# Running the experts on half of the tokens at a time, the first half under the attention of the second

## The chip, the cores and the metric

The kernel runs on one core of a Trainium2 chip. The metric is the device time of the core in microseconds; the time before is 399.92 us, the median of three runs (399.46 to 400.68). A run of one core is called slow when it is more than 1.5% above the fastest run of the same kernel; ratios use the other runs alone.

In the profile, PE is TensorE (PEld its weight loads), DVE is VectorE, ACT is ScalarE, POOL is GpSimd and SP is SyncE, which here only issues DMAs. An engine's name with a q is its sequencer, which issues DMAs in program order. L405 is line 405 of the kernel in question.

## The reference

A block-sparse attention with 8 x 8 sorted blocks feeds a mixture of experts with one expert per token.

```python
# q, k, v: (4, 8, 768, 64) fp32;  sort_net: (4, 8, 8, 8);  8 blocks of 96 rows
P = sort_net
for _ in range(5):                      # alternating row and column normalisation
    P = P - P.max(-1); P = exp(P); P = P / P.sum(-1); P = P / P.sum(-2)
k_sorted = einsum('bhij,bhjcd->bhicd', P, k_blocks)     # v_sorted the same way
attn = softmax(q_blocks @ k_sorted^T / 8)               # each block against its own sorted block
x = (attn @ v_sorted) as (3072 tokens, 512)
for e in range(8):                      # domain_id: (3072,), about 384 tokens an expert
    out[domain_id == e] = relu(x[domain_id == e] @ w1[e]) @ w2[e]   # 512 -> 1024 -> 512
```

q, k and v are 18.9 MB of fp32, the weights 33.6 MB of fp32, the output 6.3 MB. The kernel computes in fp16.

## The kernel before

The attention works on 16 "pairs" (one batch, two heads). q, k and v are loaded by DMAs of GpSimd that cast to fp16 on the way. The result x stays in SBUF, transposed, four values of a token side by side. Only when all of it is there do the experts begin. For each expert, GpSimd gathers up to 448 columns of x with its own instruction, in two halves:

```python
def x_tr(p):                                   # attention, per pair
    ...                                        # 8 transposes on TensorE
    nc.scalar.copy(xT[:, b * 768:(b + 1) * 768, hp], o.rearrange("p i c -> p (i c)"))
# [cut: loads, tables of slots, scores, softmax]

def gather(e):
    xg = moe.tile([128, CAP, 4], FP16, tag="xg", name="xg")          # CAP = 448
    for s in range(2):
        nc.gpsimd.indirect_copy(xg[:, s * 224:(s + 1) * 224, :], xT, gidx[:, e, s * 14:(s + 1) * 14],
                                i_know_this_is_slow=True)
    return xg

def up(e, xg):
    for fc in range(8):
        ...
        for dc in range(4):
            nc.tensor.matmul(h_ps, w1e[:, dc, fc * 128:(fc + 1) * 128], xg[:, :, dc],   # stride of 4 elements
                             start=(dc == 0), stop=(dc == 3))
        nc.scalar.activation(hT[:, fc], h_ps, func=AF.Relu)

def put(o_ps, col):
    o_sb = ob.tile([128, 512], FP32, tag="osb", name="o_sb")
    nc.vector.tensor_copy(o_sb, o_ps)
    nc.gpsimd.indirect_dma_start(out, ..., o_sb, None, ...)          # scatter of 128 rows
# [cut: down, and a loop of further rounds for experts with more tokens than CAP; it runs zero times here]
```

The softmax here doesn't subtract the row's maximum and nothing guards it: scores larger than these inputs give would overflow.

Of the kernel before, what the change touches and what calls it, by code (L numbers as in the profile page):

```python
# [11 lines left out]
U16 = mybir.dt.uint16  # L12
# [6 lines left out]
NE, CAP, NC16 = 8, 448, 28  # L19
NTOK = 3072  # L20
OOB = 4096


@with_exitstack
def kernel(
# [12 lines left out]
    ORDERED = {ENG.PE, ENG.Activation, ENG.DVE, ENG.Pool}  # L38

    sm = ctx.enter_context(tc.tile_pool(name="sm", bufs=1))  # L40
    wpool = ctx.enter_context(tc.tile_pool(name="wp", bufs=5))
    keep = ctx.enter_context(tc.tile_pool(name="keep", bufs=1))

    gtab = nc.dram_tensor("gtab", (128, NC16), U16, kind="Internal")
    stab = nc.dram_tensor("stab", (128, NC16), I32, kind="Internal")


    xT = keep.tile([128, NTOK, 4], FP16, tag="xT")

    attn = ExitStack()  # L50
    stg = attn.enter_context(tc.tile_pool(name="stg", bufs=2))
# [3 lines left out]
    def loads(b, h0, h1, tiles):  # L55
        for src, t in zip((k, v, q), tiles):
            nc.gpsimd.dma_start(
                t[:, h0:h1, :],
                src[b, h0:h1].rearrange("h (p t) d -> p h (t d)", t=6),
            )  # L60

    def stage_tiles():
        return tuple(stg.tile([128, NH, 384], FP16, tag=t, name=t) for t in ("kst", "vst", "qst"))

    stage = {}


    sn = sm.tile([32, 64], FP32, tag="sn")
    nc.sync.dma_start(sn, sort_net.rearrange("b h i j -> (b h) (i j)"))
    d_raw = sm.tile([128, 48], I32, tag="draw")  # L70
    nc.sync.dma_start(d_raw, moe_domain_id.bitcast(I32).rearrange("(p x) -> p x", p=128))


    with tc.manual_schedule(engines={ENG.Pool}):
        stage[0] = stage_tiles()
        loads(0, 0, 2, stage[0])
        idf16 = sm.tile([128, 128], FP16, tag="idf16")
        make_identity(nc, idf16)
        loads(0, 2, 4, stage[0])
        iota_m = sm.tile([128, 128], I32, tag="iotam")  # L80
        nc.gpsimd.iota(iota_m, pattern=[[1, 128]], base=0, channel_multiplier=0)
        tri128 = sm.tile([128, 128], FP32, tag="tri128")
        make_upper_triangular(nc, tri128, 1.0, False)
        p_i = sm.tile([128, 1], I32, tag="pi")
        nc.gpsimd.iota(p_i, pattern=[[1, 1]], base=0, channel_multiplier=1)
        tok_i = sm.tile([128, 24], I32, tag="toki")
        nc.gpsimd.iota(tok_i, pattern=[[1, 24]], base=-1536, channel_multiplier=24)
        pos_i = sm.tile([128, 4, 6], I32, tag="posi")
        nc.gpsimd.iota(pos_i, pattern=[[1, 4], [16, 6]], base=-1536, channel_multiplier=4)
        loads(0, 4, 8, stage[0])  # L90
        stage[1] = stage_tiles()
        loads(1, 0, 8, stage[1])


    rs = sm.tile([32, 8], FP32, tag="rs")
    cs = sm.tile([32, 8], FP32, tag="cs")
    sn_ij = sn.rearrange("p (i j) -> p i j", j=8)
    sn_ji = sn.rearrange("p (i j) -> p j i", j=8)
    with tc.high_priority():
        for _ in range(5):  # L100
            nc.scalar.activation(sn, sn, func=AF.Exp)
            nc.vector.tensor_reduce(rs, sn_ij, axis=AX.X, op=ALU.add)
            nc.vector.reciprocal(rs, rs)
            nc.vector.tensor_tensor(sn_ij, sn_ij, rs.unsqueeze(2).to_broadcast([32, 8, 8]), op=ALU.mult)
            nc.vector.tensor_reduce(cs, sn_ji, axis=AX.X, op=ALU.add)
            nc.vector.reciprocal(cs, cs)
            nc.vector.tensor_tensor(sn_ji, sn_ji, cs.unsqueeze(2).to_broadcast([32, 8, 8]), op=ALU.mult)

        p_rep = sm.tile([32, 8, 8, 16], FP16, tag="prep")
        nc.vector.tensor_copy(p_rep, sn_ij.unsqueeze(3).to_broadcast([32, 8, 8, 16]))  # L110

        dmask = sm.tile([128, 16], FP16, tag="dmask")
        with nc.allow_low_precision("sums of one 1"):
            nc.vector.tensor_reduce(dmask, idf16.rearrange("p (j c) -> p c j", c=16), axis=AX.X, op=ALU.add)
        pt_ps = ps.tile([128, 8, 32], FP32, tag="av", bufs=2, name="pt_ps")
# [8 lines left out]
        def build_m(eng, a, b):  # L124
# [6 lines left out]
        build_m(nc.vector, 2, 8)  # L131
    build_m(nc.vector, 8, 16)
    build_m(nc.vector, 16, 32)


    iota_f = sm.tile([128, 128], FP32, tag="iotaf")
    nc.vector.tensor_copy(iota_f, iota_m)
    iota_h = sm.tile([128, 128], FP16, tag="iotah")
    nc.vector.tensor_copy(iota_h, iota_m)
    p4 = sm.tile([128, 1], I32, tag="p4")  # L140
    nc.vector.tensor_scalar(p4, p_i, 2, None, op0=ALU.arith_shift_right)
    p4f = sm.tile([128, 1], FP32, tag="p4f")
    nc.vector.tensor_scalar(p4f, p4, 80.0, None, op0=ALU.mult)

    pos_h = sm.tile([128, 24], FP16, tag="posh")
    nc.vector.tensor_scalar(pos_h, pos_i.rearrange("p a t -> p (a t)"), p4f, None, op0=ALU.add)
    tok_h = sm.tile([128, 24], FP16, tag="tokh")
    nc.vector.tensor_copy(tok_h, tok_i)
    dom_f = sm.tile([128, 24], FP32, tag="domf")
    nc.vector.tensor_copy(dom_f, d_raw.rearrange("p (j t) -> p j t", t=2)[:, :, 0])  # L150
    oh = sm.tile([128, NE, 24], FP32, tag="oh")
    nc.vector.tensor_tensor(oh, dom_f.unsqueeze(1).to_broadcast([128, NE, 24]),
                            iota_f[:, 0:NE].unsqueeze(2).to_broadcast([128, NE, 24]), op=ALU.is_equal)
    seg = sm.tile([128, NE, 24], FP32, tag="seg")
    nc.vector.memset(seg, 1.0)
    nc.vector.memset(seg[:, :, 0:1], 0.0)
    incl = sm.tile([128, NE, 24], FP32, tag="incl")
    nc.vector.tensor_tensor_scan(incl.rearrange("p e j -> p (e j)"), seg.rearrange("p e j -> p (e j)"),
                                 oh.rearrange("p e j -> p (e j)"), 0.0, op0=ALU.mult, op1=ALU.add)
    cnt = sm.tile([128, NE], FP32, tag="cnt")  # L160
    nc.vector.tensor_copy(cnt, incl[:, :, 23])
    ones_f = sm.tile([128, 1], FP32, tag="onesf")
    nc.vector.memset(ones_f, 1.0)
    rt_ps = ps.tile([128, 64], FP32, tag="av", bufs=2, name="rt_ps")
    nc.tensor.matmul(rt_ps[:, 0:NE], tri128, cnt, start=True, stop=True)
    nc.tensor.matmul(rt_ps[0:1, 32:32 + NE], ones_f, cnt, start=True, stop=True)
    base = sm.tile([128, NE], FP32, tag="base")
    nc.vector.tensor_copy(base, rt_ps[:, 0:NE])

    mx = sm.tile([1, 1], FP32, tag="mx")  # L170
    nc.vector.tensor_reduce(mx, rt_ps[0:1, 32:32 + NE], axis=AX.X, op=ALU.max)
    caps = sm.tile([1, 8], FP32, tag="caps")
    nc.vector.tensor_scalar(caps, iota_f[0:1, 0:8], float(CAP), float(CAP), op0=ALU.mult, op1=ALU.add)
    nc.vector.tensor_scalar(caps, caps, mx, None, op0=ALU.is_lt)
    extra_f = sm.tile([1, 1], FP32, tag="extraf")
# [324 lines left out]
```

## Time and profile before

| | before |
|---|---|
| median of the runs | 399.92 us |
| span of the profile | 398.7 us |
| first score matmul | 37.8 us |
| last x copy of the attention | about 136 us |
| experts | 138 to 391 us |
| PE busy | 236.3 us, 59% |

The page of the kernel before, part 1 (busy time and share of the span of each engine) and four rows of part 2. A row cuts the span into 40 equal slices of 10 us; each digit is the busy share in tenths, for PEclk the TensorE clock that was granted, and for DMA the mean of the 16 DMA engines.

```profile
PE 236.3 (59%) x1732; PEld 126.1 (32%) x1732; DVE 121.9 (31%) x324; ACT 106.9 (27%) x182; POOL 115.8 (29%) x138
...
PE   0034878887898305999209808910980994944950
...
POOL 8932456535700011140023214102311312212120
PEclk9999875557555556999757966985895797995995
DMA  8999619999997000017601661760100100100110
```

Read the rows together: from slice 14 on PE alternates between full and empty, and the DMA engines are mostly idle. The experts have neither TensorE nor the DMA engines as their limit.

Three groups of part 5 of that page. The columns are line, engine and operation, output and input with their shape and number, then busy us and mean ns of one, then the idle time of the engine just before them and what ended most of it.

```profile
L415 PE MATMUL h_ps<-xg,w1e 128*128 128x448 f16 x256 | 102.6, 574 | 98.7 <-POOL xg L405 98.7
...
L405 POOL INDIRECT_COPY xg<-xT,gidx 128x896 f16 x16 | 19.2, 1203 | 143.7 <-issue 143.7
L423 POOL DMA_INDIRECT out_dram<-o_sb,sidx x28 | 28.1, 1005 | 62.5 <-DMA out_dram<-o_sb,sidx 28.8
```

TensorE waits 98.7 us for gathered tokens. The gathers look cheap, 1.2 us each, but 143.7 us of GpSimd lie idle just before them, put down to "issue" (33.5 us before the first, 7.3 to 7.4 before each of the other fifteen). The timeline of GpSimd (start, duration, instruction, and in brackets the idle time before it) shows how that time lies:

```profile
152.44 1.19 POOL L405 INDIRECT_COPY xg<-xT,gidx 128x896 f16 x1 [7.34 <-issue]
160.96 1.19 POOL L405 INDIRECT_COPY xg<-xT,gidx 128x896 f16 x1 [7.32 <-issue]
169.47 1.19 POOL L405 INDIRECT_COPY xg<-xT,gidx 128x896 f16 x1 [7.32 <-issue]
170.85 1.12 POOL L423 DMA_INDIRECT out_dram<-o_sb,sidx  x1 [0.19 <-DVE o_sb L422]
174.51 1.02 POOL L423 DMA_INDIRECT out_dram<-o_sb,sidx  x1 [2.54 <-issue]
```

A gather costs 8.5 us of GpSimd, a scatter comes about 3.5 us after the one before. Two gathers and three and a half scatters per expert make 29.3 us, and eight experts 235 us. GpSimd is the limit of this stage, though its row shows it a fifth busy.

### The profile page before, as it was taken

What the parts mean: (1) busy time and instruction counts of PE and PEld (TensorE: products, weight loads), DVE (VectorE), ACT (ScalarE), POOL (GpSimd) and SP (SyncE); (2) the same over time, 40 slices, a digit from 0 to 9 for tenths busy, and PEclk for the clock granted to TensorE, in tenths of its full rate; (3) what the DMA queues carried; (4) which work ended last, traced back from release to release, by engine and by line L of the source; (5) the groups of instructions that cost most, each with busy time, mean ns of one, the idle gap of its engine ahead of it and who ended that gap; (6) DMA issues with size and microseconds to landing.
All of it is one profiled execution on the core that took longest, in us unless ns stands there. A gap on an engine that the chain in (4) does not pass through costs nothing. (4 is left out here: it accounts for less than half of the span.)

```text
span 398.7 us, 4513 instructions
## 1 busy us (share of the span) xinstructions
PE 236.3 (59%) x1732; PEld 126.1 (32%) x1732; DVE 121.9 (31%) x324; ACT 106.9 (27%) x182; POOL 115.8 (29%) x138
## 2 busy tenths in 40 slices
PE   0034878887898305999209808910980994944950
PEld 0023667676777201333002302300230231311320
DVE  6998877677766200011100200110020020020020
ACT  2001676677666501222002102200210210301300
POOL 8932456535700011140023214102311312212120
PEclk9999875557555556999757966985895797995995
DMA  8999619999997000017601661760100100100110
GB/s 112 187 179 161 87 3 178 209 210 194 190 198 124 0 0 2 0 53 132 96 9 59 121 114 53 125 101 5 54 28 0 69 9 28 60 0 26 51 55 28
DMA packets 30810, 32.98 MB, mean 83 GB/s; under 512 B 4671, under 2 KB 25151, under 8 KB 30784
## 3 DMA queue, kind: packets, MB, share of 16 engines
q0 software_dynamic: 27360, 32.51, 45.6%
q1 hardware_dynamic: 3424, 0.13, 0.6%
q8 instruction: 15, 0.25, 0.2%
q14 instruction: 11, 0.09, 0.1%
HBM read 52.53 MB, written 7.36 MB: 150 GB/s over the span
## 5 line engine op out<-in xcount | busy, mean ns | idle before, releaser
L415 PE MATMUL h_ps<-xg,w1e 128*128 128x448 f16 x256 | 102.6, 574 | 98.7 <-POOL xg L405 98.7
L417 ACT ACTIVATE hT<-h_ps 128x448 f16<-128x448 f32 x64 | 34.8, 544 | 206.9 <-PE h_ps L415 206.9
L422 DVE COPY o_sb<-o_ps 128x512 f32<-128x512 f32 x28 | 19.4, 692 | 232.0 <-PE o_ps L431 227.3
L415 PEld LDWEIGHTS <-w1e 128*128 128x128 f16 x256 | 30.0, 117 | 168.1 <-issue 167.5
L405 POOL INDIRECT_COPY xg<-xT,gidx 128x896 f16 x16 | 19.2, 1203 | 143.7 <-issue 143.7
L423 POOL DMA_INDIRECT out_dram<-o_sb,sidx x28 | 28.1, 1005 | 62.5 <-DMA out_dram<-o_sb,sidx 28.8
L431 PE MATMUL o_ps<-w2e,hT 128*128 128x512 f16 x192 | 42.9, 380 | 0.0
L348 ACT COPY xT<-x_ps 128x768 f16<-128x768 f16 x16 | 29.9, 1867 | 10.5 <-PE x_ps L347 10.3
L340 DVE TENSOR_TENSOR xr<-av_ps,rc 96x256 f16<-96x256 f32 x64 | 26.9, 421 | 2.2
L277 PE MATMUL kv_ps<-M,kvx 128*128 128x128 f16 x192 | 24.2, 291 | 4.9 <-DVE M L125 4.9
L263 POOL COPY kvx<-kst 128x768 f16<-128x768 f16 x16 | 13.7, 854 | 46.2 <-PE kv_ps L277 42.0
L431 PEld LDWEIGHTS <-hT 128*128 128x128 f16 x192 | 19.0, 99 | 25.3 <-issue 4.5
L277 PEld LDWEIGHTS <-kvx 128*128 128x128 f16 x192 | 17.3, 132 | 6.8 <-issue 4.9
L265 POOL COPY qx<-qst 128x768 f16<-128x768 f16 x16 | 14.2, 888 | 0.0
L356 POOL DMA_DIRECT2D w2e<-in_moe_w_dram x8 | 7.3, 908 | 22.8 <-PE o_ps L438 22.8
L264 POOL COPY kvx<-vst 128x768 f16<-128x768 f16 x16 | 13.3, 834 | 0.0
L347 PE MATMUL x_ps<-idf_86,xr 96*128 96x96 f16 x128 | 12.7, 267 | 0.6 <-DVE xr L340 0.6
L313 PE MATMUL v_ps<-idf_86,kvT_301 64*128 64x64 f16 x128 | 8.5, 221 | 7.4 <-ACT xT L348 7.4
L313 PE MATMUL v_ps<-idf_86,kvT_302 64*128 64x64 f16 x128 | 8.1, 219 | 7.6 <-ACT xT L348 7.6
L300 PE MATMUL q_ps<-idf_86,qx 128*128 128x128 f16 x96 | 12.5, 295 | 0.0
L339 DVE RECIPROCAL rc<-av_ps 96x4 f32<-96x4 f32 x64 | 11.0, 171 | 3.2 <-PE av_ps L336 2.8
L347 PEld LDWEIGHTS <-xr 96*128 96x128 f16 x128 | 10.6, 136 | 0.8 <-DVE xr L340 0.8
(129 smaller groups left out, 257.1 us busy)
## 6 DMA issues: line engine op xcount, KB each, us to landing
w1e<-in_moe_w_dram POOLq DMA_DIRECT2D x8, 1024.0 KB, 9.4
w2e<-in_moe_w_dram POOLq DMA_DIRECT2D x8, 1024.0 KB, 14.4
kst<-in_k_dram POOLq DMA_DIRECT2D x3, 768.0 KB, 7.2
vst<-in_v_dram POOLq DMA_DIRECT2D x3, 768.0 KB, 10.2
qst<-in_q_dram POOLq DMA_DIRECT2D x3, 768.0 KB, 14.0
out_dram<-o_sb,sidx POOLq DMA_INDIRECT x28, 2.7
kst<-in_k_dram POOLq DMA_DIRECT2D x2, 192.0 KB, 4.6
vst<-in_v_dram POOLq DMA_DIRECT2D x2, 192.0 KB, 5.8
```

What stands on the lines that cost most here:

```text
L265: nc.gpsimd.tensor_copy(qq, qs[:, h].rearrange("p h (t d) -> p t h d", d=D))
L277: nc.tensor.matmul(o[:, s].rearrange("p i c -> p (i c)"), kv[:, t, h], M[:, bh].rearrange("p i c -> p (i c)"), start=True, stop=True)
L313: nc.tensor.transpose(o[:, i], kt[r, c0:c0 + 128], idf16[r, r])
L340: nc.vector.tensor_tensor(xr[p][:, 4 * ih:4 * ih + 4, h * D:(h + 1) * D], o[0:BLK, :, 0:D], rc.unsqueeze(2).to_broadcast([BLK, 4, D]), op= ...
L347: nc.tensor.transpose(o[:, i], xr[p][:, i], idf16[0:BLK, 0:BLK])
L348: nc.scalar.copy(xT[:, b * 768:(b + 1) * 768, hp], o.rearrange("p i c -> p (i c)"))
L405: nc.gpsimd.indirect_copy(xg[:, s * 224:(s + 1) * 224, :], xT, gidx[:, e, s * 14:(s + 1) * 14], i_know_this_is_slow=True)
L415: nc.tensor.matmul(h_ps, w1e[:, dc, fc * 128:(fc + 1) * 128], xg[:, :, dc], start=(dc == 0), stop=(dc == 3))
L417: nc.scalar.activation(hT[:, fc], h_ps, func=AF.Relu)
L422: nc.vector.tensor_copy(o_sb, o_ps)
L423: nc.gpsimd.indirect_dma_start(out, bass.IndirectOffsetOnAxis(ap=sidx[:, col:col + 1], axis=0), o_sb, None, bounds_check=NTOK - 1, oob_is_ ...
L431: nc.tensor.matmul(o_ps, hT[:, fc, m * 128:(m + 1) * 128], w2e[:, fc], start=(fc == 0), stop=(fc == 7))
```

## The change

The intent is to take the gather off GpSimd and to use the DMA engines and TensorE, which idle in turns. x is now written to DRAM as rows, in two halves of 1536 tokens (batches 0 and 1, and batches 2 and 3). An expert's tokens of one half (at most 224 in a round) are fetched as rows by two DMA gathers and transposed on TensorE. Such a "unit" of half and expert needs only half of the attention, so that seven of the sixteen run in pairs 9 to 15, between the matmuls of the second half's attention. q, k and v are loaded as fp32 by the SP queue and cast by GpSimd. The order of all engines' instructions, now also SP's, is that of the program.

The diff is long; this is its core, with cuts marked.

```diff
-NE, CAP, NC16 = 8, 448, 28
-NTOK = 3072
+NE, CAP = 8, 224
+NTOK, HTOK = 3072, 1536
-    ORDERED = {ENG.PE, ENG.Activation, ENG.DVE, ENG.Pool}
+    ORDERED = {ENG.PE, ENG.Activation, ENG.DVE, ENG.Pool, ENG.SP}
+    x_half = [nc.dram_tensor(f"x_half{i}", (HTOK, 512), FP16, kind="Internal") for i in range(2)]
+    def load_pair(p):                       # fp32, two staging buffers each
+        for name, src in (("kst", k), ("vst", v), ("qst", q)):
+            s = at.tile([128, 2, 384], FP32, tag=name, bufs=2, name=name)
+            nc.sync.dma_start(s, src[b, 2 * hp:2 * hp + 2].rearrange("h (p t) d -> p h (t d)", t=6))
+    def x_out(p):                           # two pairs at a time
+        nc.sync.dma_start(dst.rearrange("(i c) d -> c i d", i=8), xr2[p // 2])
+    class Unit:
+        def gather(self): ...               # 2 x nc.gpsimd.indirect_dma_start(X, None, x_half[...], ...)
+        def turn(self): ...                 # 8 transposes, one copy to xT
+        def up(self, f): ...                # 32 matmuls of 224 columns in all
+        def down(self, m): ...              # 16 matmuls of 512 columns in all
+        def put(self): ...                  # 2 scatters
# [cut: the head, the tables, the attention's inner parts]
+        W_AT = {0: 1, 2: 1, 4: 1, 6: 1, 7: 1, 8: 1, 9: 2, 10: 1, 11: 2, 12: 1}   # weight loads per pair
+        for p in range(NP):
+            if p + 2 < NP:
+                load_pair(p + 2)
+                cast_tiles(p + 2)
+                for w in "kvq":
+                    cast(p + 2, w, nc.gpsimd.tensor_copy)
+            for _ in range(W_AT.get(p, 0)):
+                load_w(*w_next.pop(0))
+            if p < 4:
+                if p == 0:
+                    build_m(nc.gpsimd, 8, 32)     # the large part of the sort matrices
+                    ranks(); places(); tables.keys()
+                tables.rows(6 * p, 6 * p + 6)
+            ue = p - 9
+            fill = first[ue].steps() if ue >= 0 else []
+            if p >= 8 and p - 8 < 7:
+                first[p - 8].gather()
+            if ue >= 1:
+                first[ue - 1].put()
+            warm = 2 if p < 8 else 0              # dummy matmuls
+            # [cut: scores, kv_bank(warm), av, q_tr, v_tr of the pairs, with fill[0..6] between them]
+            if p % 2 == 1:
+                x_out(p)
+    units = [Unit(1, e, mb) for e in range(7)] + [Unit(0, 7, mb), Unit(1, 7, mb)]
+    units[0].gather()
+    first[6].put()
+    # [cut: loads of the two weights of expert 7]
+    for n, u in enumerate(units):
+        if n + 1 < len(units):
+            units[n + 1].gather()
+        for s in u.steps():
+            s()
+        u.put()
```

## The prediction

> **What bounds it now.** Two stages run in series. The timeline shows attention with its first score matmul at 37.8 us and its last x copy done at about 136; the experts then run to 391. TensorE is busy in only 59% of the span (page, part 1). In the expert stage GpSimd's in-order queue sets the pace (timeline, chain of waits): each of 16 indirect copies takes 7.33 us of "issue" plus 1.20 us, and each of 28 scatters starts about 3.5 us after the one before (0.98 us plus a 2.53 us wait until the previous scatter to the same output landed). Per expert that is 2 x 8.53 + 3.5 x 3.5 = 29.3 us, against about 20 us of matmuls; eight experts give 235 of the 256 us. TensorE waits 98.7 us for gathers (waits). The up matmuls read x with a stride: 448 columns are paced at 0.396 us, 512 contiguous ones in the down matmul at 0.215.
>
> **What the change does.**
> - The indirect copies go (16 x 8.53 = 136 us of GpSimd). Each of 16 units (half, expert) has two DMA gathers, about 1 us of issue each, one unit ahead. This is the main gain.
> - Scatters rise from 28 to 32 and still wait for each other (the built order keeps each wait), but 14 are issued under or just after attention.
> - Up matmuls read contiguous x: an estimated 32 x 0.1 us per unit. With 16 down matmuls at 0.215 and 8 transposes a unit is 7.1 us of TensorE, plus 1 us waiting for the xT copy.
> - Seven units run in pairs 9 to 15, where a pair needs about 3.9 us of TensorE at full clock: 11 us a pair.
> - Attention loses x transposes and the 1.87 us x copy per pair (pairs took 6.5 us). Dummy matmuls should hold the clock up: it was 0.50 from 64 to 88 us and 1.00 in the dense stretch from 160 to 180. The Trainium skill, "TensorE: Matmul & The Clock Gate", Part 1, says that activity releases a throttled default; this agrees.
> - A hand-ordered head: first scores near 20 us instead of 38. The tables return as about 8 us of VectorE work in pair 0.
> - fp32 casts on GpSimd should cost as the fp16 copies did (0.83 us).
>
> **What is given back.** Weights and q, k, v are 52 MB of reads; at the 400 GB/s of 64 to 120 us that is 131 us, most of it needed before pair 12. The Trainium skill, "DMA: Bandwidth & Descriptors", "Issuing engines are not separate DMA queues", says all share the same 16 engines; so gathers queue behind weight loads (5.2 us each), most at pairs 8 to 11 and behind the last expert's load at the start of the tail.
>
> **Sum.** Head 20; pair 0 11; pairs 1 to 8 47; pairs 9 to 15 75 plus 4 of stall; write of x and first gather 6; nine tail units at 8.3, 75; stall behind the last weights 7; last scatters 7: 252 us.
>
> Predicted 252 us, 232 to 282 in 8 cases of 10. Faster by over 2%: 0.98; same 0.01; slower 0.01.
>
> **Right or wrong by:** no 7.33 us issue gaps on GpSimd; first scores at 20; pairs 1 to 8 about 5.8 us each, pairs 9 to 15 about 11; tail units 8.3 us apart; granted clock above 0.9 from pair 9; transposes waiting on gathers at pairs 10, 12 and in tail unit 1.
>
> **What would make it wrong:** a cold clock in attention (+10 us); slower fp32 casts; GpSimd, blocked on scatters behind weights, starving later casts; late gathers in every tail unit.

## The result

The changed kernel gives a correct result in 321.35 us (median of four runs, 320.39 to 323.49). The kernel before took 400.30 us on the same chip. The ratio is 0.8035, with a 95% interval of 0.799 to 0.8079: faster by 20%, where 37% had been predicted, and above the range that ended at 282. Here and below a ratio is the mean time of one kernel's fast runs over the mean of the other's fast runs of the same rounds, so it is not quite the ratio of the medians quoted beside it.

The page of the kernel after, the same lines as shown of before (a slice is now 8 us), and two lines of part 3, where each DMA queue has its packets, megabytes and its share of 16 engines' span:

```profile
PE 199.7 (63%) x2016; PEld 146.9 (46%) x2016; DVE 106.8 (34%) x251; ACT 89.9 (28%) x154; POOL 136.8 (43%) x164
...
PE   0165397678670039859519699965628988999800
...
POOL 4039766942610850437208175225413555555210
PEclk9997557755755559997957989995969999999965
DMA  6998328989999899991998824122972222222110
...
q0 software_dynamic: 16384, 26.75, 42.6%
q1 hardware_dynamic: 19520, 22.06, 21.0%
```

TensorE is empty in slices 12 and 13, counted from 0 (95 to 111 us), and thin several times after it, up to 190 us, while DMA shows 8 or 9 nearly all through this stretch. The lines of the waits view of the kernel after (engine and line, what it waited for, then us in total, times, longest) name it:

```profile
PE xt_ps L180 <- DMA X<-x_half,gidx: 52.8, 9, 22.3
POOL kvx L72 <- DMA kst<-in_k_dram: 45.9, 5, 15.0
```

TensorE waits 52.8 us for gathered rows, 39.5 us of it in pairs 9 to 15 (22.32 at once in the first). GpSimd waits 45.9 us for k. The GpSimd instructions that took the 143.7 us of issue are gone, as intended.

The stages, by the timeline of TensorE (first score matmuls of the pairs, first transposes of the units) against the prediction:

| stage | predicted us | measured us | difference |
|---|---|---|---|
| head, to the first scores | 20 | 24.2 | +4.2 |
| pair 0 | 11 | 13.8 | +2.8 |
| pairs 1 to 8 | 47 | 55.5 | +8.5 |
| pairs 9 to 15 with seven units | 75 + 4 | 118.6 | +39.6 |
| x write and first gather | 6 | 4.6 | -1.4 |
| nine tail units and the last weights | 75 + 7 | 84.5 | +2.5 |
| last matmul to the end | 7 | 16.9 | +9.9 |
| span to run time (321.35 less 318.1) | 0 | 3.3 | +3.3 |

The sum of the right column is 69.4 us, which is what 321.35 is above 252.

### The profile page after: what moved, and what is told of

The parts are those of the page before. It is cut to its first block, busy times and chain, and to the rows that moved or that the text cites. A ratio compares the mean times of both kernels' runs of the same rounds, so it can differ in the third digit from the quotient of the medians.

```text
span 318.1 us, 5081 instructions
## 1 busy us (share of the span) xinstructions
PE 199.7 (63%) x2016; PEld 146.9 (46%) x2016; DVE 106.8 (34%) x251; ACT 89.9 (28%) x154; POOL 136.8 (43%) x164
## 5 line engine op out<-in xcount | busy, mean ns | idle before, releaser
L209 POOL DMA_INDIRECT out_dram<-osb,sidx x32 | 31.5, 983 | 87.5 <-DVE xT L183 27.0
L203 DVE COPY osb<-o_ps 128x512 f32<-128x512 f32 (+1 forms) x32 | 22.1, 689 | 70.2 <-PE o_ps L200 70.2
L180 PE MATMUL xt_ps<-idf_91,X 128*128 128x128 f16 (+1 forms) x128 | 11.5, 234 | 52.8 <-DMA X<-x_half,gidx 52.8
L170 POOL DMA_INDIRECT X<-x_half,gidx x32 | 32.9, 1027 | 13.9 <-issue 6.6
L200 PEld LDWEIGHTS <-hT 128*128 128x128 f16 (+1 forms) x256 | 27.3, 110 | 22.7
L72 POOL CAST kvx<-kst 128x768 f16<-128x768 f32 x14 | 11.8, 840 | 45.9 <-DMA kst<-in_k_dram 45.9
L90 ACT CAST kvT_114<-kv_ps 128x512 f16<-128x512 f32 x23 | 13.4, 583 | 40.8 <-PE kv_ps L87 40.8
L135 DVE TENSOR_TENSOR xr<-av_ps,rc 96x512 f16<-96x512 f32 x32 | 22.0, 686 | 1.1
L90 ACT CAST kvT_115<-kv_ps 128x512 f16<-128x512 f32 x24 | 13.9, 581 | 17.8 <-PE kv_ps L87 17.8
L242 POOL TENSOR_SCALAR A<-iota_f,key 128x128 f16<-128x128 f32 x24 | 14.0, 595 | 2.0 <-DVE key L229 2.0
L122 ACT ACTIVATE E_118<-sc 96x768 f16<-96x768 f32 x10 | 8.0, 804 | 20.7 <-PE sc L119 20.7
L72 POOL CAST qx<-qst 128x768 f16<-128x768 f32 x15 | 13.0, 868 | 1.5 <-DMA qst<-in_q_dram 1.5
L122 ACT ACTIVATE E_117<-sc 96x768 f16<-96x768 f32 x11 | 8.9, 805 | 15.9 <-PE sc L119 11.7
L72 POOL CAST kvx<-vst 128x768 f16<-128x768 f32 x15 | 12.7, 844 | 1.6 <-DMA vst<-in_v_dram 1.1
## 6 DMA issues: line engine op xcount, KB each, us to landing
w_556<-in_moe_w_dram POOLq DMA_DIRECT2D x1, 1024.0 KB, 10.8
```

What stands on the lines that cost most here:

```text
L72: copy(dst, src)
L90: copy(dst[:, 4 * bank:4 * bank + 4], o)
L122: nc.scalar.activation(e[0:BLK, :, 0:4 * BLK], sc[0:BLK, :, 0:4 * BLK], func=AF.Exp, scale=0.125)
L135: nc.vector.tensor_tensor(xv, ov[:, :, :, 0:D], rc.unsqueeze(3).to_broadcast([BLK, 2, 4, D]), op=ALU.mult)
L170: nc.gpsimd.indirect_dma_start(X[0:n], None, x_half[self.half].ap(), bass.IndirectOffsetOnAxis(ap=gidx[0:n, col:col + 1], axis=0), bounds_ ...
L180: nc.tensor.transpose(o[:, dc, m * 128:m * 128 + n], self.X[m][0:n, dc * 128:(dc + 1) * 128], idf16[0:n, 0:n])
```

## The experiments

There were two theories, and a third lesser one for the head. "Supply": the 16 DMA engines cannot deliver in time what the first 200 us ask for. "Order": the data could be there, but instructions stand in the wrong order in the in-order queues of GpSimd and SP. Eighteen kernels ran, each timed in three rounds beside the kernel before. All edits are against the changed kernel unless said otherwise. The medians of the table take in slow runs (two of four in e3, e4 and h2; one in e6, e8, e9, e10, e11, f1, f3 and h4); the ratios do not, and where it matters the text gives a gain in means of fast runs too (321.6 us for the changed kernel).

| run | what differs | median us | ratio to before |
|---|---|---|---|
| the changed kernel | | 321.35 | 0.8035 |
| e1_gather_first | gathers ahead of the casts | 323.74 | 0.8081 |
| e3_one_weight (wrong) | 12 of 16 weight loads missing | 284.96 | 0.7043 |
| e5_order_all | four changes of order | 298.66 | 0.7450 |
| e6_order_one_weight (wrong) | e5 and e3 | 273.30 | 0.6800 |
| e8_ids_first | domain ids loaded first | 313.82 | 0.7837 |
| e9_m_late | large GpSimd multiply later | 317.71 | 0.7938 |
| e4_weights_early | weight loads earlier | 316.38 | 0.7847 |
| f1_order_early | e5 and e4 | 304.44 | 0.7613 |
| e2_loads_ahead | x write behind the next loads | 301.75 | 0.7526 |
| e12_scatters_split | scatters around the casts | 317.97 | 0.7937 |
| e11_no_loop | loop of further rounds left out | 314.30 | 0.7828 |
| f3_fewer_under | e5, e8, e9, five units under attention | 288.51 | 0.7192 |
| h1_swap_head | e2, e8, e9 | 300.04 | 0.7499 |
| h2_swap_one_weight (wrong) | e2 and e3 | 278.89 | fast runs 275.59, 273.90 |
| e10_no_dummies | no dummy matmuls | 324.88 | 0.8082 |
| h4_swap_head_split | e2, e8, e9, e12 | 294.16 | 0.7350 |
| f4_weights_behind_gathers | f3, weights further from gathers | 288.97 | 0.7234 |
| f5_two_gathers | h4, tail gathers two ahead | 287.92 | 0.7209 |

### Is it the order of the gathers, or the supply?

e1_gather_first moves the gather ahead of the casts in GpSimd's order:

```diff
+            if p >= 8 and p - 8 < 7:
+                first[p - 8].gather()
             if p + 2 < NP:
                 load_pair(p + 2)
                 ...                              # casts
-            if p >= 8 and p - 8 < 7:
-                first[p - 8].gather()
```

> One part: in pairs 8 to 14 the two gathers stand ahead of the casts and weight loads on GpSimd, nothing else moves. Theory A (queue order: the gathers come late because they stand behind casts that wait for q, k, v on GpSimd's in-order queue): TensorE's wait for gathers falls from 52.8 us to under 25, the stall before the first transposes from 22 us to under 8, and the time from 321 to about 300. Theory B (DMA supply: weights and q, k, v keep the 16 DMA engines full, so what lands late lands late wherever the issue stands): the wait moves from the gathers to the casts of k and to the matmuls that need them, and the time stays above 313.

It took 323.74 us, no gain. The first unit's transposes began at 109.3 us instead of 116.5, and the sum of TensorE's waits for gathers stayed (51.7 us against 52.8): the wait moved to later pairs. The order of the gathers alone is not the cause. Even ahead of the casts, the first gather left only at 103.66 us instead of 107.14 (timeline of GpSimd, e1):

```profile
103.66 1.12 POOL L170 DMA_INDIRECT X<-x_half,gidx  x1 [14.18 <-issue]
```

The view names no cause for its wait of 14.18 us, but the gather reads what the x write of pairs 6 and 7 has written. That write left at 89.05 us and took 13.8 us to land, until 102.9.

e3_one_weight uses expert 0's weights in the place of those of experts 1 to 6. Its output is wrong, which doesn't matter for the time.

```diff
             for _ in range(W_AT.get(p, 0)):
-                load_w(*w_next.pop(0))
+                e_i = w_next.pop(0)
+                wt[e_i] = wt[0, e_i[1]]
```

> Wrong result on purpose: the twelve weight loads of experts 1 to 6 are left out and all seven experts use expert 0's weights; every queue keeps its order. Theory B (DMA supply): TensorE's wait for gathers falls from 52.8 us to under 12, GpSimd's wait for k from 45.9 to under 15, time 265 to 280. Theory A (queue order): GpSimd still holds the gathers behind the casts, the wait for gathers stays above 25 us and the time above 295.

The fast runs took 281.49 and 282.92 us, 39 us less than the changed kernel's 321.65 in the mean. (Its profile is that of a slow run.) TensorE's gather waits fell to 23.3 us. So the weight traffic is a large part of the miss. That does not say yet whether the bytes or their place in a queue cost it.

e5_order_all makes four changes of order: the gather ahead of the casts, the x write behind the next loads (shown below as e2), the two scatters of a unit on either side of the casts, the weight loads last. e6 does this without the weights.

> All order changes together, right result: loads of q, k, v ahead of the write of x on the sync queue, gathers first on GpSimd, then one scatter, casts, the other scatter, and the weight loads last. Theory A: nearly the whole stall goes, time 275 to 290. Theory B: the same bytes must still land before the same units, so the gain is at most about 15 us, time above 303.

> Wrong result on purpose: the order changes of the run before and the one set of weights together. Closes the two by two. Theory A: little below the order changes alone, 270 to 288. Theory B: little below the one set of weights alone, 262 to 278, and the order is worth under 6 us once the weights are gone. If both matter, about the sum of both gains.

In means of fast runs the order brought 23.1 us (298.5), the missing weights 39.4 (282.2), both 49.2 (272.5). Neither theory is right alone, and the two losses overlap. This left open which of the four changes did it.

### The head: two small stalls

e8_ids_first loads the 24 KB of domain ids before q, k and v.

```diff
-        load_pair(0)
         d_raw = sm.tile([128, 48], I32, tag="draw")
         nc.sync.dma_start(d_raw, moe_domain_id.bitcast(I32).rearrange("(p x) -> p x", p=128))
+        load_pair(0)
```

> One part: the 24 KB of domain ids are loaded before the first q, k, v instead of behind them; nothing else moves. Head theory: VectorE's 6.3 us wait for the ids goes, they land in under 3 us instead of 8.2, the first scores come at 18 to 20 us instead of 24. If the head lies on the critical path the time falls by 4 to 6 us, to about 316; if the DMA supply sets when the experts can start, the gain is swallowed in the middle and the time stays within 2 us of 321.

The ids landed 1.7 us after their issue instead of 8.2, first scores came at 18.6 us instead of 24.2, and the time fell by 7.5 us to 313.82 (8.4 in means of fast runs).

e9_m_late moves the large sort-matrix multiply of GpSimd behind the tables.

```diff
                 if p == 0:
-                    build_m(nc.gpsimd, 8, 32)
                     ranks(); places(); tables.keys()
                 tables.rows(6 * p, 6 * p + 6)
+                if p == 0:
+                    build_m(nc.gpsimd, 8, 32)
```

> One part: GpSimd's 5.4 us multiply that builds the rest of M is issued behind the token tables' rows instead of ahead of them. Lock theory: VectorE's 128x3 cast, 5.67 us long beside that multiply, is held off by it, and falls under 0.5 us; pair 0 takes 8 to 9.5 us instead of 13.8. Rival: the cast is slow by itself or the tables' chain of small operations fills pair 0: the cast keeps its 5 us or pair 0 keeps over 12. Whole time: 317 if on the path, 321 if swallowed later.

It took 317.71 us. The reason is in two timelines of the changed kernel, the first of GpSimd, the second of VectorE:

```profile
28.15 5.37 POOL L373 TENSOR_TENSOR M<-ptb,dmask 128x3072 f16<-128x3072 f16 x1
```

```profile
27.89 5.67 DVE L409 CAST t_f<-t_i 128x3 f32<-128x3 int32 x1
33.59 0.15 DVE L411 TENSOR_SCALAR s_f<-t_f 128x1 f32<-128x1 f32 x1
```

A cast of three values per partition lasts 5.67 us and ends as the GpSimd multiply ends. In e9, with the multiply later, the timeline of VectorE has the same cast at:

```profile
28.52 0.22 DVE L409 CAST t_f<-t_i 128x3 f32<-128x3 int32 x1
```

The Trainium skill, "SBUF — State Buffer", section "SBUF: two separate sides", states that VectorE (in its two-port modes) and GpSimd take a shared pair of SBUF ports as an exclusive lock for a whole instruction, and that the other blocks fully. This agrees: 0.22 us became 5.67 beside a 5.37 us multiply. The trace does not show whether the cast ran in such a mode, and by its times the cast began 0.26 us before the multiply. Pair 0 fell from 13.8 to 7.5 us, yet only 3.6 us arrived at the end (4.2 in means of fast runs).

### Loads earlier: the stall moves

e4_weights_early only changes the table of when weights are loaded; f1 has it together with e5's order.

```diff
-        W_AT = {0: 1, 2: 1, 4: 1, 6: 1, 7: 1, 8: 1, 9: 2, 10: 1, 11: 2, 12: 1}
+        W_AT = {0: 4, 2: 1, 3: 1, 4: 1, 6: 1, 7: 1, 9: 1, 10: 1, 11: 1}
```

> One part: only the schedule of the twelve weight loads moves: four are issued in pair 0, when the DMA engines were idle by more than half, and none lies in pair 8 or 12; the bytes are the same. DMA supply theory: the queue is shorter when the gathers start, TensorE's wait for gathers falls from 52.8 to about 35 us and the time to 303 to 311. Queue order theory: the gathers still wait behind casts, time above 315.

> The order changes that gave 299 us, with the earlier weight loads. If supply and order are two separate costs the gains add: 282 to 290 us, and TensorE's wait for gathers falls from 40 to under 22 us. If the order changes had already used up what early loads can give, 295 to 299.

Two of e4's four runs were slow; the fast ones took 312.93 and 314.59 us, a gain of 7.9 us that fits neither forecast. In its profile, of a slow run, pair 9 came at 101.4 us instead of 93.5. On top of the better order the same table lost 5.5 us (304.0 against 298.5 in means of fast runs), although the gather waits fell from 40.1 to 25.1 us: GpSimd's waits for k rose from 2.6 to 16.2. Bytes that are asked for earlier push others back, as they do when the supply is full.

### One part of the order at a time

e2_loads_ahead swaps the x write and the next loads on the SP queue, and nothing else.

```diff
             if p + 2 < NP:
                 load_pair(p + 2)
+                if p % 2 == 0 and p > 0:
+                    x_out(p - 1)
 ...
-            if p % 2 == 1:
+            if p % 2 == 1 and p + 3 >= NP:
                 x_out(p)
```

> One part of the order change alone: on the loading queue each x write now stands behind the q, k, v loads of the next pair but one, instead of ahead of them. If the loads were held back by the x write waiting for its data (order), the waits for k and v on GpSimd (45.9 us in all) fall by about a third and the time is near 310; if the DMA engines are simply full (supply), it stays at 318 to 322, since the staging tiles let loads start only about 4 us earlier.

This miss was the most useful one. I had taken the swap for worth little; it brought 19.6 us (301.75), nearly all of what the four order changes bring. The timeline of SP in the changed kernel shows why:

```profile
74.15 0.33 SPq L141 DMA_DIRECT2D x_half<-xr  x1
...
88.47 0.33 SPq L141 DMA_DIRECT2D x_half<-xr  x1
88.91 0.78 SPq L61 DMA_DIRECT2D kst<-in_k_dram  x1
...
91.05 5.34 SPq L61 DMA_DIRECT2D kst<-in_k_dram  x1
```

The x write of pairs 6 and 7 can only leave when pair 7 is done, at 88.47 us. The load of k for pair 10 stands behind it in SP's order and leaves 0.44 us later, though its staging buffer was free from 82.9 us, when the cast of pair 8 had read it; the load for pair 11 follows. Two pairs' loads, an x write and a weight load are then in flight at once. This happens at every second pair, and each late load makes the next x write late. On GpSimd the late load shows in front of the first gather (timeline of GpSimd, changed kernel):

```profile
88.14 0.75 POOL L153 DMA_DIRECT2D w_1147<-in_moe_w_dram  x1
103.08 0.83 POOL L72 CAST kvx<-kst 128x768 f16<-128x768 f32 x1 [14.18 <-DMA kst<-in_k_dram]
...
105.95 0.88 POOL L156 DMA_DIRECT2D w_1255<-in_moe_w_dram  x1
107.14 1.12 POOL L170 DMA_INDIRECT X<-x_half,gidx  x1 [0.30 <-issue]
```

The cast waits 14.18 us for k, and the gather stands behind it. Without the cast it could have left some 5 us earlier at most: the x write of 88.47 landed only at 102.1. In e2 the load for pair 10 leaves at 71.06 us, ahead of the x write (timeline of SP, e2):

```profile
71.06 0.42 SPq L61 DMA_DIRECT2D kst<-in_k_dram  x1
71.62 1.50 SPq L61 DMA_DIRECT2D vst<-in_v_dram  x1
74.67 0.37 SPq L61 DMA_DIRECT2D qst<-in_q_dram  x1
77.68 0.33 SPq L141 DMA_DIRECT2D x_half<-xr  x1
```

The Trainium skill, "DMA: Bandwidth & Descriptors", section "Anatomy of one DMA — SWDGE (gpsimd) path", notes that "any semaphore wait happens on the issuing sequencer before dispatch". The section describes DMAs that GpSimd issues; that the same holds for the SP queue, where one waiting write holds every load behind it, is shown by this trace and by the swap: the write left at 88.47, the load at 88.91, and with the swap the same load left 17.9 us earlier (the sum of what had piled up to pair 10).

Pairs 1 to 8 took 43.9 us in e2 against 55.5. The table of stages for this stretch, one fence for each kernel (window in us, its length, busy us of PE, PEld, DVE, ACT and POOL with instruction counts, granted clock, DMA share, GB/s); first the changed kernel, then e2:

```profile
38.00:93.50 55.50, 43.38 (x575) 34.17 (x570) 29.08 (x73) 25.24 (x40) 31.99 (x45) 0.59 0.85 207
```

```profile
37.40:81.30 43.90, 34.82 (x575) 26.89 (x571) 28.41 (x73) 24.76 (x40) 34.73 (x47) 0.83 0.91 248
```

The same 575 matmuls are busy for 34.82 us instead of 43.38, with the clock granted at 0.83 instead of 0.59. Late loads cost twice: in the wait, and in the clock after it.

What the swap did not mend is the stall for gathers (waits view of e2):

```profile
PE xt_ps L180 <- DMA X<-x_half,gidx: 49.1, 7, 23.3
```

It was 52.8 us before the swap; in pairs 9 to 15 it is 36.0 against 39.5. Of the 20 us, 11.6 came in pairs 1 to 8 and about 5 in pairs 9 to 15. GpSimd's waits for k fell from 45.9 to 1.9 us and the first gather left 16.2 us earlier, at 90.96, but pair 9 was ready 12.2 us earlier too, and the rows landed at 105.0. The first unit waits for two transfers in turn: the x write of pairs 6 and 7, and then the gather. The write's line in the DMA view (KB, then us from issue to landing) for the changed kernel, e2, and h2, which is e2 without twelve weight loads (below):

```profile
x_half<-xr SPq DMA_DIRECT2D x1, 384.0 KB, 13.6
```

```profile
x_half<-xr SPq DMA_DIRECT2D x1, 384.0 KB, 12.4
```

```profile
x_half<-xr SPq DMA_DIRECT2D x1, 384.0 KB, 3.4
```

The weight loads are issued by GpSimd and this write by SP. That the write still lands 9 us sooner without them points to the traffic on the engines, and not to a place in GpSimd's queue.

e12_scatters_split does another part of the order alone: the first scatter of a unit ahead of the casts, the second behind them, the weight loads last.

```diff
+            if ue >= 1:
+                first[ue - 1].put((0,))        # ahead of the casts
             ...                                # casts
-            for _ in range(W_AT.get(p, 0)): load_w(*w_next.pop(0))
             ...
             if ue >= 1:
-                first[ue - 1].put()
+                first[ue - 1].put((1,))
+            for _ in range(W_AT.get(p, 0)): load_w(*w_next.pop(0))
```

> Another part of the order change alone: the two scatters of a unit stand on either side of the three casts, and weight loads come last in a pair. If a scatter that waits on GpSimd (13.7 us once, 60 us summed over all) starves the casts and through them the pairs, 308 to 314 us; if the scatter only waits for what the DMA engines have not delivered, 318 to 323 us.

It took 317.97 us, 3.4 less. With e1's nothing and e2's 19.6 this adds up to about what the four parts of e5 bring together.

e11_no_loop leaves out the loop for further rounds at the end. This is a test, not an improvement: other inputs need the loop.

```diff
-    n_extra = nc.values_load(extra_i[0:1, 0:1], min_val=0, max_val=6)
-    with tc.For_i(0, n_extra, 1):
-        ...
```

> The loop for further rounds at the end is left out; it runs zero times with these inputs, so the result is still correct, but a kernel for any input needs it. The time from the last down matmul to the end is 16.9 us, of which 4.7 us pass until the last scatter and 12.2 after it. If reading the count and stepping over the loop make up a good part of those 12.2 us, it falls to 310 to 316 us; if the end is the write landing and the program's fixed ending, it stays at 319 to 323 us.

It took 314.30 us. From the last down matmul to the end it now took 8.1 us instead of 16.9. (The profiled run was a slow one; in the mean of fast runs, 313.5 against 321.6, the gain is the same 8 us.) So reading the count and stepping over a loop that never runs cost about 8 us together. The Trainium skill, "Runtime: NRT & Kernel Launch", section "Instruction fetch mechanics", says that a taken branch out of the fetched window stalls for a fetch; the run agrees with a cost at this place and does not show its parts. The kernel before had this end too, 14 us from its last matmul; the prediction had overlooked it.

f3_fewer_under puts the lessons so far together: e5, e8, e9, only five units under the attention (pairs 11 to 15), and the weights of experts 6 and 7 loaded after it, with gathers two units ahead in the tail.

> The best version so far (298.7 us) with the domain ids loaded before q, k, v, the large sort-matrix multiply moved behind the tables, five units under the attention instead of six and a half (they start in pair 11 instead of 9), the weights of experts 6 and 7 loaded after the attention, and tail gathers two units ahead. It gives a correct result. If the supply of data up to the end of the attention is what fails (my theory), taking 4 MB out of it and starting the units two pairs later removes most of the 40 us of gather waits, and costs about two more units in the tail at 8 us against two pairs that shorten from 10.5 to about 6: 255 to 275 us, with gather waits of TensorE under 20 us in all. If only the order of the queues counts, it is 298.7 less the 10 us of the two head changes plus about 6: 290 or more.

It took 288.51 us, the best so far, but between the two forecasts. The stalls in the attention fell to one of 10.8 us and one of 3.4 (the profile is of a slow run); the tail units, with the weights of two experts now to be loaded between them, came 8 to 13 us apart.

### What is left after the swap

These runs asked whether the swap and the supply are two losses, and whether the head's gains survive. h2 is e2 and e3 together, h1 is e2, e8 and e9, h4 is h1 with e12.

> Wrong result on purpose: the x writes behind the next loads, and the weights of expert 0 used for the experts 1 to 6 as well, so that 12 of the 16 weight loads are missing. The swap alone gave 301.8 us, the missing weights alone 285.0, all four order changes with the missing weights 273.3. If late loads and lack of supply are two separate losses, both gains add: 265 to 270. If the swap mostly mends what the weights cause too, 273 to 280, near the run with all four order changes. Gather waits of TensorE should fall below 20 us.

Two of four runs were slow (282.5, 282.2), the fast ones took 275.59 and 273.90. In means of fast runs: changed kernel 321.6, swap 301.6, missing weights 282.2, both 274.7. So the swap is worth 20.1 us alone and 7.5 without the weights; the weights 39.4 alone and 26.9 after the swap. They share 12.6 us. In the run with both, pairs 10 to 15 started every 10.5 us, with no wait for a gather, and pair 9 waited 6.7 us for its own. Pairs 9 to 15 took 81.0 us in all: the predicted 75 plus 4 comes out when this traffic is missing.

> Three changes at once, each already run alone: the x writes behind the next loads (301.8 us alone), the domain ids loaded before q, k, v (gain 7.5 us alone), and the large sort-matrix multiply moved behind the tables (gain 3.6 us alone). Correct result. If the gains add, 290.5 us, 288 to 293. If the DMA engines, full from 45 to 150 us after the swap, are the limit and swallow an earlier start, 296 to 302.

It took 300.04 us: of the 11 us that the head changes bring alone, 1.7 are left after the swap (the intervals of the two ratios overlap). First scores at 21.2 us instead of 24.1 and pair 0 of 9.0 us instead of 13.3 are all there; but pair 9 came at 81.5 us against 81.3. The reason is the row of the DMA engines in h1's page, part 2 (slices of 7.5 us):

```profile
DMA  5999969999999999979857241317921222222110
```

From slice 6 to slice 17 there is hardly anything but 9. From the start of the program until the first unit's transposes the DMA share is 0.99 in e2 (105.0 us) and 1.02 in h1 (100.8 us), and 0.89 in the changed kernel (116.5 us). The table of stages has it in the last but one column, first e2, then h1:

```profile
0.00:105.00 105.00, 48.67 (x700) 35.92 (x700) 54.55 (x157) 36.13 (x59) 63.52 (x86) 0.76 0.99 247
```

```profile
0.00:100.80 100.80, 54.29 (x701) 39.34 (x702) 51.54 (x157) 36.65 (x59) 59.41 (x83) 0.72 1.02 253
```

The share can pass 1 (the kernel before has 1.19 from 64 to 120 us), so that a share near 1 is full is a reading, not a measurement. Share times length is taken here as an estimate of the engines' work: 103.7 us in the changed kernel, 104.0 in e2, 102.8 in h1. In these three the same transfers stand before the first unit, and it did not start before about 103 us of DMA work were done. In e1, e5 and h4, where the weight load of pair 8 is issued behind the first gather, it started after 93 to 95. What an earlier head gives is then taken again by the full engines. In h2, without twelve weight loads, the share is 0.74 and the unit starts at 89.6 us.

> The same as the run with the swap and both head changes, with the two scatters of a unit on either side of the casts and the weight loads last in a pair, which alone gained 3.4 us. Correct result. If these gains add too, about 287 us (284 to 290), the best so far; if the supply swallows them, 290 or more, no better than without them.

It took 294.16 us: 6 us better than h1, more than e12 alone had brought, and short of the 287 that would have been the full sum. Its first unit started at 98.2 us against 100.8 in h1.

> The changed kernel without the dummy matmuls of pairs 0 to 7 (two in each, 512 columns, meant to hold the granted clock up). If they hold the clock up, pairs 1 to 8 get slower, by 5 us or more in all: 326 us or more. If the clock follows how densely TensorE works in the pairs anyway, and the loads set their pace, 318 to 323 us, with the granted clock between 38 and 93 us at 0.59 as before.

```diff
-            warm = 2 if p < 8 else 0
+            warm = 0
```

It took 324.88 us (320.62 to 327.1), ratio 0.8082 with an interval of 0.8013 to 0.8152, which overlaps the changed kernel's 0.799 to 0.8079. An effect of the dummies on the time was not found, and one of a per cent is not excluded. The clock from pair 1 to pair 9 was 0.54, against 0.59 with them, and its mean over each of the four runs was 0.775 to 0.781, against 0.796 to 0.815: they raise it a little. In e2, where the pairs hardly wait for loads, it was 0.83.

### Gathers next to weight loads

f5_two_gathers is h4 with one thing added: tail gathers run two units ahead, which puts the second unit's gather ahead of the last expert's weight loads. f4 is f3 with each weight load placed right behind a gather rather than just ahead of the next one.

```diff
         units[0].gather()
+        units[1].gather()
         first[6].put()
 ...                                   # loads of expert 7's weights
         for n, u in enumerate(units):
-            if n + 1 < len(units):
-                units[n + 1].gather()
-            for s in u.steps(): s()
+            steps = u.steps(); steps[0]()
+            if n + 2 < len(units):
+                units[n + 2].gather()
+            for s in steps[1:]: s()
```

> The version with the swap, both head changes and the split scatters (294.2 us), with one thing added: in the tail the gathers run two units ahead, so that the second unit's gather is issued before the last expert's two weight loads instead of 2 us behind them. Correct result. In that version the first unit of the tail lasts 19 us and the second 9.6, against 8 for the others, and the second's transposes wait 7.9 us. If the place behind the weight loads is the reason, that stretch shortens by 8 to 11 us: 283 to 286 us. If something else holds it, 291 or more.

It took 287.92 us, 6.2 less than h4 (5.0 in means of fast runs), against 8 to 11 expected. The first tail unit fell from 19.1 to 10.7 us, the second rose from 9.6 to 11.6: the third gather now stands behind the weight loads and waits 3.4 us.

> The version with five units under the attention (288.5 us), with each weight load now issued well ahead of the next gather instead of just before it, and the gather of the first unit of the second half ahead of the scatters. Correct result. In that version the units from 151 to 243 us start 10 to 14 us apart against 8 for an undisturbed one, with waits for gathers of 2.3 to 3.4 us at each. If gathers wait because they stand behind weight loads in the same queue, those units close up to 8 to 9 us: 272 to 280 us. If the tail is short of supply by itself, 285 or more.

It took 288.97 us, not told apart from f3's 288.51. The first units after the attention (from 155.8, 163.8 and 171.8 us) do close up, to 8.0 us, as expected; the five after them open up to 11 to 15. The timeline of GpSimd in f4 shows where the wait went (the first line is the second gather of a unit):

```profile
168.06 0.99 POOL L170 DMA_INDIRECT X<-x_half,gidx  x1 [0.30 <-PE h_ps L192]
169.06 0.86 POOL L535 DMA_DIRECT2D wl<-in_moe_w_dram  x1
170.22 1.06 POOL L209 DMA_INDIRECT out_dram<-osb,sidx  x1 [0.30 <-issue]
179.48 0.94 POOL L209 DMA_INDIRECT out_dram<-osb,sidx  x1 [8.21 <-DVE osb L203]
180.73 1.05 POOL L170 DMA_INDIRECT X<-x_half,gidx  x1 [0.31 <-issue]
```

The scatter is now the first thing behind the weight load. The scatter after it waits for it to land and leaves 9.3 us later instead of 3.5. (The view names VectorE's copy, but the copy that this scatter sends was done at 164.7. What both waited for is seen in VectorE's timeline of f4, in the line below: its next copy needed the buffer of the scatter of 170.22, and waited for that one to land until 178.77.) The next gather stands behind both.

```profile
178.77 0.69 DVE L203 COPY osb<-o_ps 128x512 f32<-128x512 f32 x1 [5.51 <-DMA out_dram<-osb,sidx]
```

A gather that comes late also costs more than its wait. Two stretches of TensorE's timeline in f4, one undisturbed, one after a wait of 3.92 us:

```profile
165.23 3.23 PE L192 MATMUL h_ps<-xT,w 128*128 128x224 f16 x32 [0.73 <-DVE xT L183]
...
198.18 0.40 PE L180 MATMUL xt_ps<-idf,X 128*128 128x128 f16 x4 [3.92 <-DMA X<-x_half,gidx]
199.62 0.50 PE L180 MATMUL xt_ps<-idf,X 96*128 96x96 f16 x4 [1.05 <-DMA X<-x_half,gidx]
200.83 5.83 PE L192 MATMUL h_ps<-xT,w 128*128 128x224 f16 x32 [0.71 <-DVE xT L183]
```

The same 32 matmuls take 3.23 us warm and 5.83 after the wait. The Trainium skill, "TensorE: Matmul & The Clock Gate", Part 1, says that the clock falls back to half after an idle window of about 3.4 us; a wait of 3.9 us with 2.6 us of lost speed behind it agrees, the granted clock being 0.60 over that unit. But in the same run the unit that began at 212.24 us, after a wait of only 2.12 us, took 5.37 us for its matmuls at 0.58, so shorter waits can cost as much.

f3, f4 and f5 are the best versions found (0.7192, 0.7234 and 0.7209, intervals overlapping), 10% faster than the changed kernel. f5 is the simplest of them.

## Why the prediction was wrong

**What held.** The limit of the kernel before was read rightly: with the indirect copies gone, the 143.7 us of issue on GpSimd went. fp32 casts cost 0.83 us as the fp16 copies had. Tail units started 8.0 us apart (8.3 predicted), pairs with a unit took 10.5 us where nothing was late (11 predicted), and in e2, with loads in time, pairs 1 to 8 took 5.5 us each (5.8 predicted). TensorE's work was sized well where nothing was late.

**The step that failed** is the supply of data, in the prediction's words "52 MB of reads; at the 400 GB/s of 64 to 120 us that is 131 us, most of it needed before pair 12", and in the sum "pairs 9 to 15 75 plus 4 of stall". The stall was 39.5 us of waits for gathers instead of 4, and pairs 1 to 8 lost another 8.5. Three things were wrong in it.

- The work was undercounted. In the first 210 us of the changed kernel the DMA share is 0.81, thus an estimated 170 us of work; in e2 it is 0.86 of 195 us, 168 us. The prediction's 131 us must be put in the same unit. In the stretch from which its 400 GB/s were read (kernel before, 64 to 120 us), the queue of the weights alone had this line in the DMA view (packets, MB, share of 16 engines):

```profile
q0 software_dynamic: 9103, 11.13, 117.9%
```

  Without the last expert's two loads, which come later, the prediction has about 121 us (131 less 2 x 5.2); at a share of 1.179 these are an estimated 143 us of work. Some 25 us were left out: the prediction counted reads of weights, q, k and v alone, and also on the engines were eight x writes, fourteen gathers and up to as many scatters. A weight load was sized rightly: 5.2 us at that share are 6.1 of work, and from the 168 us of e2, at the end of its attention, to the 95 of h2 (0.58 of 164) with twelve loads less, it is an estimated 6 each.
- The path to the first unit was left out of the stall. For the second half the sum has "write of x and first gather 6" (4.6 measured); for the first half it has nothing. There the x write of pairs 6 and 7 left at 88.47 us, 5 us before pair 9, and landed 13.6 us later, and the gather, which left at 107.14, needed 9.3 more to land. This was the longest wait, 22.3 us. Without twelve weight loads (h2) the write landed in 3.4 us and the wait was 6.7.
- The supply was taken as an average, though the queue before it was not steady. On SP each x write held the loads of the next two pairs until its own pairs were done. From 32 to 48 us the engines had nearly idle slices (3 and 2 in tenths), then everything left at once. The prediction had considered the order of the computing engines only; SP, which does no computing, became an in-order queue with this change, and its order alone cost 20 us, most of it in pairs 1 to 8. The gather stall stayed when this was mended (36.0 us in pairs 9 to 15 of e2).

The prediction did name that "gathers queue behind weight loads", and a wait of 10.3 us lies at pair 12 and one of 8.0 in the second tail unit, where it looked for them; the longest, 22.3, lies at pair 9, where it did not. But most of 131 us of work was to be done before pair 12, which by its own sum (20 + 11 + 47 + 3 x 11) began at 111 us. Ahead of the first gather alone stood eight weight loads and q, k and v of eleven pairs, 29.8 MB: at its own 400 GB/s an estimated 74 us, and pair 9 was to begin at 78. There was no slack in this, and 4 us could not have been right. A sum of that kind must be laid against the time in which it has to be done.

**Other terms.** The head was 4.2 us longer since 24 KB of ids stood behind q, k and v (e8). Pair 0 was 2.8 us longer since GpSimd's multiply held VectorE (e9). The end was 9.9 us longer, about 8 of it the loop that is stepped over (e11); the trace of before showed this end and it had not been read. The clock in attention was, as the prediction feared, cold: 0.59 from pair 1 to 8. Its remedy, the dummy matmuls, raised the clock by 0.05 there and was not seen to gain time (e10); loads that come in time did both (e2). And "granted clock above 0.9 from pair 9" failed with the waits: it was 1.00 from 130 to 140 us, between stalls, and 0.50 at 110 to 120, after the longest.

**What stays open.** With the swap, both head changes and the split scatters, 294.16 us, there are still gather waits in pairs 9 to 15. That they come from the amount of data alone is supported by h2, by the full DMA row and by the x write that lands 9 us sooner without the weights, though it is not in their queue. But the missing weights also take away the place that they hold in GpSimd's queue ahead of the gathers; for the gathers themselves no run parts the two. Nor is the predicted 252 us shown to be reachable: even with twelve weight loads missing and a wrong result the kernel needed 273.

## What to carry to other kernels

When a change makes a DMA queue ordered by program, read that queue as one would an engine: a store that waits for its data holds every load behind it, so put the loads first. Before hiding one stage under another, add up all transfers that must land in the shared stretch, writes and gathers too, and lay them against its length; where they fill it, gains ahead of it are swallowed, and moving loads only moves the stall. Where a stage's input goes through DRAM, put the landing of the write, and of the read behind it, into the sum at the length that they have among the other traffic (13.6 and 9.3 us here). A late operand costs TensorE its wait and then its clock.

## What the Trainium skill lacked or had wrong

- "DMA: Bandwidth & Descriptors" has no figure for a load that casts. In the kernel before, from 64 to 120 us, the weight queue moved 11.13 MB of fp16, read as twice as many bytes of fp32: an estimated 397 GB/s (2 x 11.13 MB over 56 us), with this one core at work. Its Specifications give about 358 GB/s as the limit of HBM for one core; the same page says below its table of measured loads that those were taken with the other core of the pair idle and go higher, so 397 does not contradict it.
- The same page, "Anatomy of one DMA", says where a wait is held, but none of its rules says that a store in front of loads on one issuing engine holds them. "Perfetto Trace Analysis", section "DMA Optimizations", does advise one engine for inputs and another for outputs, for the sake of spread. The stronger reason is this one: it cost 20 us here (321.35 to 301.75). A second issuing engine for the x writes was not tried.
- The same page gives a fixed cost of about 2.0 us to a DMA of GpSimd's path and no figure for one among others: from SP, 24 KB of ids landed 1.7 us after issue ahead of q, k and v, and 8.2 us behind them; 384 KB of x took 12.4 us among weight loads (e2) and 3.4 without most of them (h2).
- "TensorE: Matmul & The Clock Gate", Part 1, says that activity releases the clock and names a busy window of about 3.4 us, but not how dense such a window has to be. Two dummy matmuls of 512 columns in each of eight pairs left it at 0.59 (0.54 without); pairs that did not wait had 0.83.
- "GPSIMD Engine Reference" has no cost for the indirect copy of 224 columns of four: 1.2 us busy in each of 16, and 7.3 to 7.4 us of issue before it in all but the first.
- "Runtime: NRT & Kernel Launch", "Instruction fetch mechanics", gives no figure for the stall of a taken branch. Reading a count and stepping over a loop of zero rounds at the end cost about 8 us together here (16.9 to 8.1 us from the last matmul to the end).
